# Retention, then a squared-ReLU layer: q of the first four pairs in 2 KB rows, clusters joined from the fifth group on, and the order planned anew

## The chip, the core and the metric

The kernel runs on one core of a Trainium2 chip. The metric is device time in microseconds of one execution, from the first instruction to the last. TensorE multiplies matrices, VectorE and ScalarE do elementwise work and read what TensorE leaves in PSUM, GpSimd does elementwise work in SBUF and issues some DMAs, and SyncE issues the other DMAs. Each engine takes its instructions in the order of the program and waits where an operand isn't there.

## The reference

```python
B, H, S, D = 8, 8, 576, 64
scores = (q @ k.transpose(0, 1, 3, 2)) / sqrt(D)
gamma = 1.0 - 2.0 ** (-5.0 - arange(H))
rel = pos[:, None] - pos[None, :]
Dmat = where(rel >= 0, gamma ** rel, 0.0)
x = (scores * Dmat) @ v                  # causal, with decay: retention
x = x.transpose(0, 2, 1, 3).reshape(B * S, H * D)      # 4608 x 512
out = (maximum(x @ w_in, 0.0) ** 2) @ w_out            # 512 -> 2048 -> 512
```

Inputs and output are float32. The kernel computes in float16 with float32 sums.

## The kernel before

**Units, groups, pairs.** The 4608 rows are cut into 36 units of 128 rows: 128 positions of one batch, or the last 64 positions of two batches (a tail). Two units make a group, so there are 18 groups. The first eight units, groups 0 to 3, are handled as four pairs: 256 neighbouring positions of one batch, named after their first unit (0, 2, 4, 6).

**Retention.** For each group: scores of k and q (`psc`), masked by VectorE into `rx` (pairs) or `rT` (later groups); sums of k times v (`psS`), from which VectorE makes the running states `stmp`, `R` and `Rm`; and outputs (`psO`) from the masked scores times v and q times the state. VectorE multiplies `psO` by the decay into `xT`, the input of the layer. These matmuls use quarter tiles of the array (64x64), so a cluster of them stands between full-tile matmuls, with a change before and after it.

**How k and q get transposed.** For pairs, k and q are loaded into `pair`, cast to float16 (`kx`, `qx`, two casts each), transposed by TensorE (`psT`) and copied to `kqT`. From unit 8 on, GpSimd casts them to `kq` and a DMA transposes `kq` into `kqT`. v is cast with a decay factor, to `vx` (pairs) or `v`.

**The layer.** `ph` is `xT` times w_in; ScalarE makes `rl` (ReLU) and mostly also the square `gT`; VectorE does a few squares. `po` is `gT` times w_out: plainly for group 0 (128x512 matmuls), and by a scheme of seven products instead of eight for the rest (128x256 matmuls, with `gS`, sums of `gT`, and `wT`, differences of w_out, made by VectorE).

**Loads.** All on the same DMA engines: k, q and v of pairs 0 and 2; then eight pieces of the weights, 512 KB each, issued by GpSimd (w0 to w3 of w_in, w4 to w7 of w_out); then pairs 4 and 6, k of pair 4 being held back by `behind` until w5 has landed; then units 8 and on. A pair's load is 512 KB. Before, partition p of all three held positions 2p and 2p+1 of each head, in runs of 512 bytes.

**What sets the order.** The program's order is not written by hand. A class `Schedule` plays the whole kernel through as a list of tasks, each with an engine, a key (smallest first among those ready), a duration, the resources that it takes, and its users; and emits the instructions of all engines in the order of that play. So a changed duration moves instructions on all engines. `LAG` adds to the landing times of some loads in that play, `WARM` is the number of matmuls on junk data that keep TensorE busy ahead of the real work, and `JOIN` says from which group on the output of one group and the scores of the next share a cluster:

```python
def joined(g):
    return JOIN <= g < last_g
...
f1: emit_out1(g); emit_scores(g + 1)     # q times the old state, and scores of the next group
f2: emit_sums(g + 1); emit_out2(g)       # sums of the next group, and the rest of the output
```

A group that is not joined runs scores and sums in one cluster and its output in another, with a drain between the output's halves. With JOIN at 5 the fifth group (number 4) is the last one of that kind, the final group aside.

Of the kernel before, what the change touches and what calls it, by code (L numbers as in the profile page):

```python
# [9 lines left out]
FP32 = mybir.dt.float32  # L10
# [5 lines left out]
class Schedule:  # L16
# [6 lines left out]

    def add(self, eng, key, dur, fn, deps=(), acq=(), after=None, lag=0.0):
        t = dict(eng=eng, key=key, dur=dur, fn=fn, acq=acq, n=len(self.tasks), users=[], free=[], lag=lag,
                 left=len(deps), ready=0.0, lat=self.LAT[eng] if after is None else after)
        for d in deps:
            d["users"].append(t)
        self.tasks.append(t)
        return t  # L30
# [11 lines left out]
    def emit(self):  # L42
        ready = {e: [] for e in self.LAT}
        busy = {e: False for e in self.LAT}
        events = []
        order = []
        seq = 0

        def push(at, what, t):
            nonlocal seq  # L50
            seq += 1
            heapq.heappush(events, (at, seq, what, t))
        for t in self.tasks:
            if t["left"] == 0:
                heapq.heappush(ready[t["eng"]], (t["key"], t["n"], t))
        now = 0.0
        while True:
            for e in ready:
                if busy[e]:
                    continue  # L60
                held = []
                while ready[e]:
                    item = heapq.heappop(ready[e])
                    t = item[2]
                    if all(self.count[r] >= t["acq"].count(r) for r in t["acq"]):
                        for r in t["acq"]:
                            self.count[r] -= 1
                        t["start"] = now
                        order.append(t)
                        busy[e] = True  # L70
                        push(now + t["dur"], "end", t)
                        break
                    held.append(item)
                for item in held:
                    heapq.heappush(ready[e], item)
            if not events:
                break
            now = events[0][0]
            while events and events[0][0] <= now + 1e-9:
                _, _, what, t = heapq.heappop(events)  # L80
                if what == "end":
                    busy[t["eng"]] = False
                    for w in t["users"]:
# [20 lines left out]
def kernel(  # L104
# [105 lines left out]

    mask2 = const.tile([P, 2, 2, 64], FP32, name="mask2")
    nc.gpsimd.memset(mask2, 1.0)
    for c in range(2):
        for e in range(2):
            m = mask2[c * 64:(c + 1) * 64, e]
            nc.gpsimd.affine_select(out=m, in_=m, compare_op=ALU.is_ge, fill=0.0, base=-e, pattern=[[1, 2], [2, 64]],  # L216
                                    channel_multiplier=-2)
# [6 lines left out]
    L = 2 * NF  # L224
    WARM = 34
    EARLY = 20
    SQ_ACT = (0, 1, 2, 3, 4, 5, 6)
    SPREAD = 0.1
    QL = 0.8
    BESIDE = 1.1  # L230
    PAUSE = 1.5
# [3 lines left out]
    SQ_LATE = (1, 4, 6)  # L235
    JOIN = 5
    LAG = {"k4": 0.7, "q4": 0.5}
    LAG_T, LAG_O = 1.5, 5.0
# [69 lines left out]
    def add_load_pair(name, u):  # L308
        n = "kqv".index(name)

        def fn():
# [3 lines left out]
            b, c = units[u][1:]  # L315
            t = nc.sync.dma_start(out=x, in_=(k, q, v)[n][b, :, c * P:(c + 2) * P, :].rearrange("h (p e) d -> p h (e d)", e=2))
            if (name, u) == ("k", 4):
                behind(t, tile_of["w", 5])
            tile_of["load", name, u] = t
        loaded[name, u] = loaded[name, u + 1] = dma_task(0, 1.81 if loaded else 2.9, fn, acq=("wst",) if name != "q" else (),  # L320
                                                         after=2.1 + LAG.get(name + str(u), 0.0))

    issues = []

    def add_weight(i):
# [9 lines left out]
        issues.append(issue)  # L335
        t = add("SP", 0, 2.75, lambda: None, deps=last_load + [issue], after=2.1 + LAG.get(f"w{i}", 0.0))
        last_load[:] = [t]
# [65 lines left out]
    def add_unit_pair(u, base):  # L403
# [4 lines left out]
        for i, name in enumerate("kqv"):  # L408
            xs[name] = []
            for e in range(2):  # L410
                eng = ("DVE" if (e if name == "v" else lead) else "ACT" if name == "k" and u >= 4 or u == 2 and e else
                       "DVE" if name == "q" and u == 2 else "POOL")

                def fc(name=name, e=e, eng=eng):
# [4 lines left out]
                    if name == "v":  # L419
                        (nc.vector if eng == "DVE" else nc.gpsimd).tensor_tensor(  # L420
                            out=t.rearrange("p (h d) -> p h d", d=D), in0=x,
                            in1=vdec[f"pair{e}"].rearrange("p (h o) -> p h o", o=1).to_broadcast([P, H, D]), op=ALU.mult)
                    else:
                        engines[eng](out=t.rearrange("p (n b a d) -> p n b a d", n=2, b=2, a=2),
# [9 lines left out]
        for i, name in enumerate("kq"):  # L434
# [9 lines left out]
            for s in range(2):  # L444
                on_act = i == 0 or s == 0 or u > 0

                def fe(i=i, s=s, on_act=on_act):
                    if i == 0:
                        tile_of["kqT", u + s] = work.tile([P, 2 * NP, P], FP16, name="kqT", tag="kqT", bufs=6)
                    (nc.scalar.copy if on_act else nc.vector.tensor_copy)(  # L450
                        out=tile_of["kqT", u + s][:, i * NP:(i + 1) * NP].rearrange("p x (e t) -> p e x t", e=2),
                        in_=tile_of["psT", u, i][:, :, :, half(s)])
                es.append(add("ACT" if on_act else "DVE", base + 3 + i + s / 2, 0.66, fe, deps=[t] + T["kqT", u + s],
# [14 lines left out]
    def add_ret_pair(g):  # L468
# [7 lines left out]
        for e in range(2):  # L476
# [11 lines left out]
            for a in range(2):  # L488
                def fm(e=e, a=a):
                    nc.vector.tensor_tensor(  # L490
                        out=rT[e][:, a], in0=rT["ps", e][a].rearrange("p (n i) -> p n i", i=P),
                        in1=mask2[:, e].rearrange("p (o e) i -> p o (e i)", o=1).to_broadcast([P, NP, P]), op=ALU.mult)
                ms.append(add("DVE", base + 5 + e, 0.66, fm, deps=[t] + ms))
# [79 lines left out]
        for s in range(2):  # L573
            def fx(s=s):
                if s == 0:
                    tile_of["x", g] = x_pool.tile([P, NP, 2 * P], FP16, name="xT", tag="xT")
                nc.vector.tensor_tensor(
                    out=tile_of["x", g][:, :, s * P:(s + 1) * P].rearrange("p n (i e) -> p n e i", e=2),
                    in0=tile_of["psO", g][s].rearrange("p (n e i) -> p n e i", n=NP, e=2),
                    in1=gam_f.rearrange("p n (i e) -> p n e i", e=2), op=ALU.mult)  # L580
            T["x", u + s] = add("DVE", base + 25 + s, 0.7, fx, deps=[t] + ([T["x", u]] if s else []), acq=() if s else ("x",))
# [119 lines left out]
    def after_sums(g, t, key, res):  # L701
# [23 lines left out]
        r1 = add("DVE", key + 0.2 - URGENT, 0.69, fr1, deps=[r0])  # L725
        r2 = add("DVE", key + 0.3, 0.65, fr2, deps=[r1], acq=("R",))
        T["Rm", g], T["R", g], T["Rread", g], T["Rmread", g] = r0, r2, [], r1
# [94 lines left out]
    def add_wT(i, in0, in1):  # L822
        ts = []
        for h in range(2):
            def f(h=h):
                sl = slice(h * HF // 2, (h + 1) * HF // 2)
                nc.vector.tensor_tensor(out=wT[i][:, sl], in0=in0[:, sl], in1=in1[:, sl], op=ALU.subtract)
            ts.append(add("DVE", WT_KEY + i, 0.7, f, deps=sum((wcast[j] for j in range(4, 8 if i else 6)), [])))
        return ts
# [5 lines left out]
    for x, y in ((t2, t1), (t4, t2)):  # L835
        for p in y:
            for w in x:
                sched.need(w, p)
    wT_done = {7: t3, 6: t2, 5: t1, 4: t4}
# [18 lines left out]
    def add_ff(g):  # L858
# [10 lines left out]
        for fb in range(NF // nf):  # L869
# [18 lines left out]
            def fg(fb=fb, on_act=on_act):  # L888
# [6 lines left out]
                else:  # L895
                    nc.vector.tensor_tensor(out=t, in0=rl, in1=rl, op=ALU.mult)  # L896
            r = add("ACT", place(4 * fb + 4), 0.6, fr, deps=[f1[-1]], acq=("rl",))
            sched.free("ff", [r])
            sq.append(add("ACT" if on_act else "DVE", place(4 * fb + 6), 0.63 if on_act else 0.55, fg, deps=[r] + sq[:1],
                          acq=() if fb else ("g",)))  # L900
            sched.free("rl", [sq[-1]])
# [30 lines left out]
    def add_strassen(g, us, base, sq):  # L932
# [7 lines left out]
        def add_sum(k, key, parts, in0, in1, op, deps, start=()):  # L940
            out_ = []
            for h in range(parts):
                def f(sl=cut(parts, h)):
                    if ("S", g) not in tile_of:
                        tile_of["S", g] = stage.tile([P, 4, HF, P], FP16, name="gS", tag="wst")
                    nc.vector.tensor_tensor(out=tile_of["S", g][:, k, sl], in0=in0(sl), in1=in1(sl), op=op)  # L946
                out_.append(add("DVE", key + h, (BESIDE if h else 0.5) if parts > 1 else 0.8, f, deps=deps(h, parts) + list(start)))
            sums[k] = out_
# [163 lines left out]
```

## Time and profile before

| | |
|---|---|
| time, median of 3 | 289.84 us (289.72 to 289.88) |
| span of the profiled execution | 288.5 us |
| TensorE busy | 280.7 us, 97% |
| ScalarE, VectorE, GpSimd busy | 187.5, 177.7, 87.1 us |
| DMA engines, share of the time by windows | 1.20 from 5 to 12 us, 0.97 from 100 to 200 us |
| matmuls of the layer, busy | ph 136.6 us; po in five groups, 135.8 us in sum |

Matmuls are pipelined: one of 128x256 is shown with 273 ns, but the next starts 109 ns after it. So the time of a stretch of matmuls is read from start to start, and a hole shows as a start that comes too late. The profile counts a stretch as idle from 150 ns on.

### The profile page before, as it was taken

The page shows a single profiled execution, that of the slowest core. Times are in us where ns is not written, and L with a number is a line of the kernel's source. Part 1 is how long each engine was busy: PE and PEld are TensorE (multiplying, and loading weights), DVE is VectorE, ACT ScalarE, POOL GpSimd, SP SyncE. Part 2 cuts the span into 40 slices and gives each one's busy share as a digit, 9 for nine tenths or more (in the row PEclk, how much of TensorE's full clock was granted, in tenths as well). Part 3 has the DMA queues.
Part 4 walks back from the last instruction along what each step waited for, and adds up shares of the span by engine and source line. Part 5 has one row for each costly group of instructions (what it writes and reads, how often), then busy time and mean ns, then how long its engine had stood idle before and what let it go on. Part 6 is the DMA issues. An engine that isn't in the chain of part 4 may idle for free.

```text
span 288.5 us, 10135 instructions
## 1 busy us (share of the span) xinstructions
PE 280.7 (97%) x4346; PEld 236.0 (82%) x4346; DVE 177.7 (62%) x341; ACT 187.5 (65%) x363; POOL 87.1 (30%) x124
## 2 busy tenths in 40 slices
PE   7999999999999999999999999999999999999994
PEld 2568767888888888888888888888888888888883
DVE  3772389868466756657666574767666566364632
ACT  5558975667584757667575748675848665847830
POOL 5660045433525243423325151534433100000000
PEclk9999999999999999999999999999999999999999
DMA  7999999999999898989898997989899420102004
GB/s 202 275 208 206 248 277 267 168 240 144 212 222 186 210 201 216 179 214 168 222 146 197 231 185 182 220 200 248 177 160 228 110 75 5 73 2 75 0 2 145
DMA packets 122156, 49.94 MB, mean 173 GB/s; under 512 B 94720, under 2 KB 117760, under 8 KB 122112
## 3 DMA queue, kind: packets, MB, share of 16 engines
q1 hardware_dynamic: 117568, 44.84, 71.0%
q0 software_dynamic: 4224, 4.19, 8.8%
q8 instruction: 34, 0.56, 0.8%
q10 hardware_dynamic: 320, 0.26, 0.4%
q14 instruction: 10, 0.08, 0.1%
HBM read 36.70 MB, written 9.44 MB: 160 GB/s over the span
## 4 chain that ended last, share of the span: by engine, by line
PE 88%; DMA 3%; DVE 3%; POOL 2%; issue 2%; DVEq 0%; POOLq 0%
PE ph L876 43%; PE po L973 36%; PE psO L357 4%; DMA w_in<-in_moe_w_in_dram 3%; PE po L916 2%; PE psS L357 2%; PE psc L357 2%; DVE rx L490 1%; DVE o L996 1%; DVE gS L946 1%; POOL mask L216 0%; DVE vx L420 0%; POOL vx L420 0%; POOL w_in L331 0%; PE psT L439 0%
## 5 line engine op out<-in xcount | busy, mean ns | idle before, releaser
L876 PE MATMUL ph<-xT,w_in 128*128 128x256 f16 x1152 | 136.6, 273 | 0.3 <-DMA w_in<-in_moe_w_in_dram 0.3
L876 PEld LDWEIGHTS <-w_in 128*128 128x128 f16 x1152 | 111.4, 98 | 14.7 <-DMA w_in<-in_moe_w_in_dram 0.6
L884 ACT ACTIVATE rl<-ph 128x512 f16<-128x512 f32 x144 | 84.3, 586 | 50.7 <-PE ph L876 48.1
L894 ACT ACTIVATE gT<-rl 128x512 f16<-128x512 f16 x118 | 74.4, 631 | 3.4
L973 PEld LDWEIGHTS <-gS 128*128 128x128 f16 x544 | 51.7, 98 | 6.5
L973 PE MATMUL po<-wT,gS 128*128 128x256 f16 x408 | 55.8, 273 | 0.0
L946 DVE TENSOR_TENSOR gS<-gT,gS 128x512 f16<-128x512 f16 (+1 forms) x51 | 31.3, 613 | 24.2 <-ACT gT L894 23.7
L973 PEld LDWEIGHTS <-gT 128*128 128x128 f16 x408 | 39.6, 98 | 4.8
L973 PE MATMUL po<-w_out,gT 128*128 128x256 f16 x272 | 36.8, 273 | 0.0
L387 POOL TENSOR_TENSOR v<-v,vdec_full 128x512 f16<-128x512 f32 x24 | 26.6, 1108 | 28.1 <-DMA v<-in_v_dram 24.4
L371 POOL CAST kq<-k 128x512 f16<-128x512 f32 x28 | 19.7, 702 | 36.9 <-DMA k<-in_k_dram 31.2
L946 DVE TENSOR_TENSOR gS<-gT 128x1024 f16<-128x1024 f16 x34 | 24.7, 726 | 6.4 <-ACT gT L894 6.3
L382 POOL CAST kq<-q 128x512 f16<-128x512 f32 x24 | 15.6, 649 | 32.0 <-DMA q<-in_q_dram 31.8
L896 DVE TENSOR_TENSOR gT<-rl 128x512 f16<-128x512 f16 x26 | 11.8, 455 | 20.1 <-ACT rl L884 20.1
L996 DVE TENSOR_TENSOR o<-po,u 128x256 f32<-128x256 f32 x33 | 13.9, 422 | 15.3 <-PE po L973 7.7
L986 ACT COPY u<-po 128x256 f32<-128x256 f32 x34 | 12.5, 368 | 15.7 <-PE po L973 15.5
L751 DVE TENSOR_TENSOR xT<-psO,gam_full 128x512 f16<-128x512 f32 x28 | 18.0, 685 | 3.8 <-PE psO L357 3.6
L996 DVE TENSOR_TENSOR o<-po,p 128x256 f32<-128x256 f32 x18 | 7.6, 424 | 20.6 <-ACT u L986 12.7
L973 PE MATMUL po<-w_out,gS 128*128 128x256 f16 x136 | 18.0, 273 | 0.0
L692 DVE TENSOR_TENSOR rT<-psc,mask_full 128x512 f16<-128x512 f32 x24 | 15.6, 685 | 3.7 <-PE psc L357 3.2
L973 PE MATMUL po<-wT,gT 128*128 128x256 f16 x136 | 17.6, 273 | 0.0
L1047 ACT COPY o<-po 128x256 f32<-128x256 f32 x16 | 5.9, 370 | 10.8 <-PE po L973 9.1
(82 smaller groups left out, 227.1 us busy)
## 6 DMA issues: line engine op xcount, KB each, us to landing
out_dram<-o SPq DMA_DIRECT2D x32, 256.0 KB, 3.0
k<-in_k_dram SPq DMA_DIRECT2D x24, 256.0 KB, 4.5
q<-in_q_dram SPq DMA_DIRECT2D x96, 64.0 KB, 3.2
v<-in_v_dram SPq DMA_DIRECT2D x24, 256.0 KB, 3.5
pair<-in_k_dram SPq DMA_DIRECT2D x4, 512.0 KB, 7.0
pair<-in_q_dram SPq DMA_DIRECT2D x4, 512.0 KB, 6.1
pair<-in_v_dram SPq DMA_DIRECT2D x4, 512.0 KB, 6.6
w_in<-in_moe_w_in_dram POOLq DMA_DIRECT2D x4, 512.0 KB, 9.2
```

Source lines behind the costliest of these rows:

```text
L357: t = nc.tensor.matmul(out_, lhsT=lhsT, rhs=rhs, start=start, stop=True, skip_group_check=True, tile_position=(64 * row, 64 * col))
L371: op(out=out_.rearrange("p (n b a d) -> p n b a d", n=2, b=2, a=2), in_=in_.rearrange("p (a n b) d -> p n b a d", n=2, a=2))
L382: nc.gpsimd.tensor_copy(out=tile_of["kq", u][:, 1].rearrange("p (t a d) -> p a t d", t=4, a=2), in_=tile_of["q32", u].rearrange("p (a t) d ...
L387: nc.gpsimd.tensor_tensor(out=t, in0=tile_of["v32", u], in1=vdec[kind].rearrange("p (h o) -> p h o", o=1).to_broadcast([P, H, D]), op=ALU. ...
L692: tile_of["masking", g] = nc.vector.tensor_tensor(out=tile_of["rT", g][:, :, a], in0=tile_of["psc", g][a].rearrange("p (s n i) -> p s n i" ...
L751: nc.vector.tensor_tensor(out=tile_of["x", g].rearrange("p n (s e i) -> p e (n s) i", s=n, e=2)[:, c], in0=y.rearrange("p (o t r) -> p o r ...
L876: nc.tensor.matmul(tile_of["ph", g, fb][:, j, :], lhsT=w_in16[:, m, fi * P:(fi + 1) * P], rhs=tile_of["x", g][:, m, :], start=(m == 0), st ...
L884: nc.scalar.activation(out=t, in_=tile_of["ph", g, fb], func=ACTF.Relu)
L894: nc.scalar.activation(out=t, in_=rl, func=ACTF.Square)
L946: nc.vector.tensor_tensor(out=tile_of["S", g][:, k, sl], in0=in0(sl), in1=in1(sl), op=op)
L973: nc.tensor.matmul(tile_of["pb", g, bank], lhsT=left(i), rhs=right[:, i, :], start=(start and i == 0), stop=(i == HF - 1), skip_group_chec ...
L996: nc.vector.tensor_tensor(out=o_tile(u)[:, half * HM:(half + 1) * HM], in0=bank(x), in1=tile_of[name, g], op=ALU.add)
```

## The change

**q of the pairs.** The eight heads are split in two halves of four, and each half is one DMA: partition p holds 8 neighbouring positions of one head, p = 4 * (block of 8 positions) + head within the half. Each row is 2 KB in one run. The positions of q are thereby in another order, so the cast to `qx`, the copy of q to `kqT`, the mask `mask2` and the write of `xT` take other strides. k and v are loaded as before.

**Join.** JOIN goes from 5 to 4, so group 4 shares clusters with group 5.

**Order.** The planner gets other figures: VectorE's operations with two SBUF operands (`soft`) run at a `SHARED` rate of 0.22 beside a long GpSimd task, and faster otherwise; loads of q, weights and some landings have other durations; the differences `wT` are released half by half; `HURRY` puts a few tasks of group 1 first; and there are 26 warm-up matmuls instead of 34. For pair 2, ScalarE now does all casts of k and q, where GpSimd, VectorE and ScalarE shared them.

```diff
-    def add(self, eng, key, dur, fn, deps=(), acq=(), after=None, lag=0.0):
+    SHARED = 0.22
+    def add(self, eng, key, dur, fn, deps=(), acq=(), after=None, lag=0.0, soft=False):
...
+        def shared(beside):
+            t = port["task"]
+            if t is not None:
+                port["left"] -= (now - port["at"]) * (self.SHARED if port["beside"] else 1.0)
+                port["at"] = now
+                t["end"] = now + max(port["left"], 0.0) / (self.SHARED if beside else 1.0)
+                push(t["end"], "end", t)
+            port["beside"] = beside
...
-    WARM = 34
+    WARM = 26
-    BESIDE = 1.1
+    HURRY = 60
-    JOIN = 5
-    LAG = {"k4": 0.7, "q4": 0.5}
+    JOIN = 4
+    LAG = {"k0": 0.3, "w7": 1.4, "v6": 1.2}
...
-            t = nc.sync.dma_start(out=x, in_=(k, q, v)[n][b, :, c * P:(c + 2) * P, :].rearrange("h (p e) d -> p h (e d)", e=2))
+            src = (k, q, v)[n][b, :, c * P:(c + 2) * P, :]
+            if name == "q":
+                for a in range(2):
+                    t = nc.sync.dma_start(out=x[:, NP * a:NP * a + NP].rearrange("p t d -> p (t d)"),
+                                          in_=src.rearrange("(a x) (r t) d -> a r x (t d)", a=2, t=8)[a])
+            else:
+                t = nc.sync.dma_start(out=x, in_=src.rearrange("h (p e) d -> p h (e d)", e=2))
...
-        loaded[name, u] = loaded[name, u + 1] = dma_task(0, 1.81 if loaded else 2.9, fn, ...
+        loaded[name, u] = loaded[name, u + 1] = dma_task(0, 2.9 if not loaded else 1.41 if name == "q" else 1.81, fn, ...
...
-        t = add("SP", 0, 2.75, lambda: None, deps=last_load + [issue], after=2.1 + LAG.get(f"w{i}", 0.0))
+        t = add("SP", 0, 2.58, lambda: None, deps=last_load + [issue], after=3.0 + LAG.get(f"w{i}", 0.0))
...
-                eng = ("DVE" if (e if name == "v" else lead) else "ACT" if name == "k" and u >= 4 or u == 2 and e else
-                       "DVE" if name == "q" and u == 2 else "POOL")
+                eng = ("DVE" if (e if name == "v" else lead) else "ACT" if name == "k" and u >= 4 or u == 2 and name != "v" else "POOL")
...
+                    elif name == "q":
+                        x = tile_of["q32", u].rearrange("p (a t) (s d) -> p a (t s) d", a=2, s=2)[:, :, NP * e:NP * e + NP]
+                        engines[eng](out=t.rearrange("p (t a d) -> p a t d", t=NP, a=2), in_=x)
...
+                    out_, in_ = tile_of["kqT", u + s][:, i * NP:(i + 1) * NP], tile_of["psT", u, i]
+                    if i == 0:
+                        out_, in_ = out_.rearrange("p x (e t) -> p e x t", e=2), in_[:, :, :, half(s)]
+                    else:
+                        out_ = out_.rearrange("p x (t r) -> p t x r", r=16)
+                        in_ = in_.rearrange("p e y (r x) -> p (e y) x r", x=NP)[:, :, :, 16 * s:16 * s + 16]
...
-                    out=tile_of["x", g][:, :, s * P:(s + 1) * P].rearrange("p n (i e) -> p n e i", e=2),
-                    in0=tile_of["psO", g][s].rearrange("p (n e i) -> p n e i", n=NP, e=2),
+                    out=tile_of["x", g][:, :, s * P:(s + 1) * P].rearrange("p n (r t) -> p n r t", t=8),
+                    in0=tile_of["psO", g][s].rearrange("p (n t r) -> p n r t", n=NP, t=8),
...
-            ts.append(add("DVE", WT_KEY + i, 0.7, f, deps=sum((wcast[j] for j in range(4, 8 if i else 6)), [])))
+            ts.append(add("DVE", WT_KEY + i, 0.68, f, deps=wcast[4 + h] + (wcast[6 + h] if i else []), soft=True))
```

More of the change, by code (lines that the diff above doesn't have):

```diff
@@ L22, in __init__ @@
         self.tasks = []
-    def add(self, eng, key, dur, fn, deps=(), acq=(), after=None, lag=0.0):
-        t = dict(eng=eng, key=key, dur=dur, fn=fn, acq=acq, n=len(self.tasks), users=[], free=[], lag=lag,
+    SHARED = 0.22
+    def add(self, eng, key, dur, fn, deps=(), acq=(), after=None, lag=0.0, soft=False):
+        t = dict(soft=soft, eng=eng, key=key, dur=dur, fn=fn, acq=acq, n=len(self.tasks), users=[], free=[], lag=lag,
                  left=len(deps), ready=0.0, lat=self.LAT[eng] if after is None else after)
@@ L56, in emit @@
         now = 0.0
+        port = dict(task=None, left=0.0, at=0.0, beside=False)
+        def shared(beside):
[6 more added lines that the diff above has]
+            port["beside"] = beside
         while True:
@@ L70, in emit @@
                         busy[e] = True
-                        push(now + t["dur"], "end", t)
+                        t["end"] = now + t["dur"]
+                        if t["soft"]:
+                            port.update(task=t, left=t["dur"], at=now)
+                            shared(port["beside"])
+                        else:
+                            push(t["end"], "end", t)
+                        if e == "POOL" and t["dur"] > 0.5:
+                            shared(True)
                         break
@@ L81, in emit @@
                 if what == "end":
+                    if abs(t["end"] - now) > 1e-6:
+                        continue
+                    t["end"] = -1.0
                     busy[t["eng"]] = False
+                    if t["soft"]:
+                        port["task"] = None
+                    elif t["eng"] == "POOL" and t["dur"] > 0.5:
+                        shared(False)
                     for w in t["users"]:
@@ L209 @@
                                     compare_op=ALU.is_ge, fill=0.0, base=0, pattern=pattern, channel_multiplier=-1)
-    mask2 = const.tile([P, 2, 2, 64], FP32, name="mask2")
+    mask2 = const.tile([P, 2, 8, 16], FP32, name="mask2")
     nc.gpsimd.memset(mask2, 1.0)
@@ L215 @@
             m = mask2[c * 64:(c + 1) * 64, e]
-            nc.gpsimd.affine_select(out=m, in_=m, compare_op=ALU.is_ge, fill=0.0, base=-e, pattern=[[1, 2], [2, 64]],
+            nc.gpsimd.affine_select(out=m, in_=m, compare_op=ALU.is_ge, fill=0.0, base=-e, pattern=[[1, 8], [8, 16]],
                                     channel_multiplier=-2)
@@ L319, in fn @@
             tile_of["load", name, u] = t
-        loaded[name, u] = loaded[name, u + 1] = dma_task(0, 1.81 if loaded else 2.9, fn, acq=("wst",) if name != "q" else (),
+        loaded[name, u] = loaded[name, u + 1] = dma_task(0, 2.9 if not loaded else 1.41 if name == "q" else 1.81, fn, acq=("wst",) if name != "q" else (),
                                                          after=2.1 + LAG.get(name + str(u), 0.0))
@@ L449, in fe @@
                         tile_of["kqT", u + s] = work.tile([P, 2 * NP, P], FP16, name="kqT", tag="kqT", bufs=6)
-                    (nc.scalar.copy if on_act else nc.vector.tensor_copy)(
-                        out=tile_of["kqT", u + s][:, i * NP:(i + 1) * NP].rearrange("p x (e t) -> p e x t", e=2),
-                        in_=tile_of["psT", u, i][:, :, :, half(s)])
+                    out_, in_ = tile_of["kqT", u + s][:, i * NP:(i + 1) * NP], tile_of["psT", u, i]
+                    if i == 0:
+                        out_, in_ = out_.rearrange("p x (e t) -> p e x t", e=2), in_[:, :, :, half(s)]
+                    else:
+                        out_ = out_.rearrange("p x (t r) -> p t x r", r=16)
+                        in_ = in_.rearrange("p e y (r x) -> p (e y) x r", x=NP)[:, :, :, 16 * s:16 * s + 16]
+                    (nc.scalar.copy if on_act else nc.vector.tensor_copy)(out=out_, in_=in_)
                 es.append(add("ACT" if on_act else "DVE", base + 3 + i + s / 2, 0.66, fe, deps=[t] + T["kqT", u + s],
@@ L491, in fm @@
                         out=rT[e][:, a], in0=rT["ps", e][a].rearrange("p (n i) -> p n i", i=P),
-                        in1=mask2[:, e].rearrange("p (o e) i -> p o (e i)", o=1).to_broadcast([P, NP, P]), op=ALU.mult)
+                        in1=mask2[:, e].rearrange("p (o t) r -> p o (t r)", o=1).to_broadcast([P, NP, P]), op=ALU.mult)
                 ms.append(add("DVE", base + 5 + e, 0.66, fm, deps=[t] + ms))
@@ L577, in fx @@
                 nc.vector.tensor_tensor(
-                    out=tile_of["x", g][:, :, s * P:(s + 1) * P].rearrange("p n (i e) -> p n e i", e=2),
-                    in0=tile_of["psO", g][s].rearrange("p (n e i) -> p n e i", n=NP, e=2),
-                    in1=gam_f.rearrange("p n (i e) -> p n e i", e=2), op=ALU.mult)
+                    out=tile_of["x", g][:, :, s * P:(s + 1) * P].rearrange("p n (r t) -> p n r t", t=8),
+                    in0=tile_of["psO", g][s].rearrange("p (n t r) -> p n r t", n=NP, t=8),
+                    in1=gam_f.rearrange("p n (r t) -> p n r t", t=8), op=ALU.mult)
             T["x", u + s] = add("DVE", base + 25 + s, 0.7, fx, deps=[t] + ([T["x", u]] if s else []), acq=() if s else ("x",))
@@ L725, in after_sums @@
         r1 = add("DVE", key + 0.2 - URGENT, 0.69, fr1, deps=[r0])
-        r2 = add("DVE", key + 0.3, 0.65, fr2, deps=[r1], acq=("R",))
+        r2 = add("DVE", key + 0.3, 0.62, fr2, deps=[r1], acq=("R",), soft=True)
         T["Rm", g], T["R", g], T["Rread", g], T["Rmread", g] = r0, r2, [], r1
@@ L835 @@
     for x, y in ((t2, t1), (t4, t2)):
-        for p in y:
-            for w in x:
-                sched.need(w, p)
+        for w, p in zip(x, y):
+            sched.need(w, p)
     wT_done = {7: t3, 6: t2, 5: t1, 4: t4}
@@ L896, in fg @@
                     nc.vector.tensor_tensor(out=t, in0=rl, in1=rl, op=ALU.mult)
-            r = add("ACT", place(4 * fb + 4), 0.6, fr, deps=[f1[-1]], acq=("rl",))
+            r = add("ACT", place(4 * fb + 4) - HURRY * (g == 1 and fb == 7), 0.6, fr, deps=[f1[-1]], acq=("rl",))
             sched.free("ff", [r])
-            sq.append(add("ACT" if on_act else "DVE", place(4 * fb + 6), 0.63 if on_act else 0.55, fg, deps=[r] + sq[:1],
-                          acq=() if fb else ("g",)))
+            sq.append(add("ACT" if on_act else "DVE", place(4 * fb + 6) - HURRY * (g == 1 and not on_act), 0.63 if on_act else 0.43, fg, deps=[r] + sq[:1],
+                          acq=() if fb else ("g",), soft=not on_act))
             sched.free("rl", [sq[-1]])
@@ L946, in f @@
                     nc.vector.tensor_tensor(out=tile_of["S", g][:, k, sl], in0=in0(sl), in1=in1(sl), op=op)
-                out_.append(add("DVE", key + h, (BESIDE if h else 0.5) if parts > 1 else 0.8, f, deps=deps(h, parts) + list(start)))
+                out_.append(add("DVE", key + h - HURRY * (g == 1), 0.43 if parts > 1 else 0.72, f, deps=deps(h, parts) + list(start), soft=True))
             sums[k] = out_
```

## The prediction

> **What bounds the kernel now.** I read the page first, for shares; then the list of who waited for whom on the matmul engine; then the chain of waits in the one stretch that is not solid; then the timelines of the engines that feed it.
>
> ```profile
> PE 280.7 (97%) x4346; PEld 236.0 (82%) x4346; DVE 177.7 (62%) x341; ACT 187.5 (65%) x363; POOL 87.1 (30%) x124
> PE   7999999999999999999999999999999999999994
> PEclk9999999999999999999999999999999999999999
> ```
>
> TensorE is the bound, at full clock, and no other engine comes near. So an edit is worth only what it takes from the matmul stream or from the holes in it. All of TensorE's holes are early:
>
> ```profile
> PE psT L439 <- DVE kx L424: 0.8, 1, 0.8
> PE psS L357 <- POOL vx L420: 0.3, 1, 0.3
> PE ph L876 <- DMA w_in<-in_moe_w_in_dram: 0.3, 1, 0.3
> PE psS L357 <- DVE vx L420: 0.3, 1, 0.3
> ```
>
> The first two lie before 12 us, where warm-up matmuls are run anyway. The third is where real work begins. The timeline of TensorE there, and of GpSimd, which issues the weight DMAs:
>
> ```profile
> 17.73 1.92 PE L876 MATMUL ph<-xT,w_in 128*128 128x256 f16 x16
> 19.97 1.48 PE L876 MATMUL ph<-xT,w_in 128*128 128x256 f16 x12 [0.33 <-DMA w_in<-in_moe_w_in_dram]
> ```
> ```profile
> 10.94 0.81 POOL L331 DMA_DIRECT2D w_in<-in_moe_w_in_dram  x1
> ```
> ```profile
> DMA to landing us min/median/max: 9.0/9.0/9.0
> ```
>
> The second piece of w_in is issued at 10.94 and lands 9.0 us later, at 19.94; TensorE restarts at 19.97. From there to 49.3 it never stops, so the date of that landing sets all that follows. The wait has nothing to do with the issue: six loads are ahead of the weights, and the windows view has the DMA engines full (share 1.20 and 290 GB/s from 5 to 12 us, 207 GB/s of weights from 14 to 32 us).
>
> The fourth hole is in the chain of waits:
>
> ```profile
> 43.33 0.44 PE psS L357 x32
> ...
> 47.18 0.68 DVE rx L490
> 47.86 0.33 DVE o L996
> 48.19 0.60 DVE gS L946
> 48.79 1.03 DVE vx L420
> 49.81 0.04 issue
> 49.86 0.41 PE psS L357 x28
> ```
>
> Here the chain leaves TensorE for 6 us of VectorE work: R, stmp, four rx masks, and only then vx of pair 6, for which psS of group 3 waits. Start to start, the fourth psS matmul costs 0.52 us more than its neighbours, and one psc after it (50.96) 0.16 more. After 51 us every start-to-start step is either a plain matmul (109 ns for 128x256) or the change between full and quarter tiles.
>
> **What the Trainium skill says.** "DMA: Bandwidth & Descriptors", section "Why small descriptors are slow (HBM only)", names a fixed cost per packet and per descriptor, so longer runs move faster. The trace agrees: 512-byte loads move at 299 GB/s (3 to 12 us), while the two stretches filled by 2 KB stores show 380 and 366 GB/s. "GPSIMD Engine Reference", the table that lists SBUF interfaces, has GpSimd and VectorE share theirs when VectorE has two SBUF inputs. The trace agrees: the gS subtraction of 1024 takes 0.68 us alone and 1.53 beside a GpSimd multiply at 68.27; the first qx cast at 39.05 took 0.86 instead of 0.61 beside gS. "TensorE: Matmul & The Clock Gate", section "What's actually happening", has the array fall to half clock after an idle window of about 3.4 us; here only the start shows it (11 warm-ups in 4.32 us, 0.39 each, against 0.22 later). "VectorE: DVE Perf Modes", section "Mode 2×_1P", wants step 1 for packed 16-bit reads, which bears on one small copy below.
>
> **The change part by part.** Total matmul work is the same; only eight warm-ups go. I compared the order of instructions of both kernels engine by engine.
>
> *q0 and q2 in 2 KB rows.* Each 512 KB load of 512-byte rows takes 1.8 us (landings at 4.99, 6.78, 8.59, 10.39). In 2 KB rows it is 256 packets; the stores' packets took 87 to 90 ns each, so 256 x 88 / 16 = 1.4 us; by rate, 0.524 MB at 366 GB/s is 1.43. The two q loads ahead of the weights save 2 x 0.4 = 0.8 us (0.4 to 0.9). Every weight piece queues behind them and lands earlier by that: the restart moves from 19.97 to 19.2. For this, the matmuls before must be ready: xT of group 0 ended at 15.95 against a first ph at 17.73, and the masks of group 1 at 19.94 against psO at 21.39. Both have more than 0.8 us in hand, and q's casts of pair 2 moved to ScalarE have it idle there. One kqT copy on VectorE now reads with step 4; it may go from 0.42 to the 0.68 of an unpacked read. That 0.26 lies in the same slack. **-0.8.**
>
> *The order between 22 and 42 us.* In the new order psT of k4 and q4 is moved ahead of eight of the po matmuls of 512 (8 x 0.216 = 1.73), and psT of q4 also ahead of ten po of 256 (10 x 0.109 = 1.09). So TensorE asks for qx of pair 4 2.82 us earlier, relative to the restart. Before, the two GpSimd casts ended at 40.52 (39.05 plus 1.47) and psT began at 41.85: slack 1.33. The shortfall is 2.82 - 1.33 = 1.49, about 1.52 with a release of 0.03. What comes back: q4 itself is 0.4 shorter, and the casts may need 2 x 0.61 = 1.22 instead of 1.47. The restart's 0.8 cancels, since k4 is queued behind w5 and moves with it. This leaves 1.52 - 0.4 - 0.25 = 0.87 us in which TensorE stands, with po, psS and all later work behind it in its queue (bounds: 0, if pair 4 gets more of the DMA engines beside the last weights; 1.1, if q4 gains only 0.3 and the casts stay slow). k's casts on ScalarE ended at 39.11 against psT at 40.31; 1.73 earlier they are short by 0.5, but they waited for ScalarE until 37.97 with k4 landed at 37.08, and the new order puts them right behind the last rl. I count them at nothing. **+0.87.**
>
> *psS of group 3.* Between psS of group 2 and of group 3 stand now 46 po of 256 and two of 512, where there were 24 of 256; and VectorE does the masks straight after stmp, then xT, o and vx. From psS of group 2: 1.1 us of R and stmp, masks to about 4.2, R and wT to 5.3, xT after psO to 7.0, o and vx to about 8.3; TensorE needs about 9.3. The hole of 0.52 and the 0.16 go. **-0.68.**
>
> *More cuts.* psc now stands alone where it followed psO, so there is one more change to quarter tiles and back: 0.09 + 0.14. **+0.24.** Joining from group 4 merges its clusters with those of group 5, but the number of clusters from group 4 on stays 28; what goes is the drain between its halves (0.27 at 68.07). **-0.27.**
>
> *The rest.* Masks, xT and casts with other strides keep their counts of elements and their f32 PSUM reads (0.68 each); xT and rx are off the path by the paragraphs above. The planner's new figures for shared SBUF access change no instruction. The last 220 matmuls stand in the old order. Cost nothing.
>
> Sum: -0.8 + 0.87 - 0.68 + 0.24 - 0.27 = -0.64, so 289.84 - 0.64 = **289.2 us**.
>
> **The rivals.** (a) *q4 is in time.* The 0.87 falls away: 288.3. For it: the last weights and pair 4 share the engines, and whichever gets more decides; q4 needs only 0.9. Against: bytes queued before the end of q4 are fixed. (b) *The load gain is small and the stall full.* q saves 0.2 each: -0.4 + 1.1 - 0.4 + 0.24 - 0.27 = +0.3 at the worst, 289.6 to 290.1: no difference. For it: stores are not loads. (c) *A new wait, slower.* Joining group 4 asks for psc of group 5 at about 71 us instead of 77.3, and its DMA transpose (issued 67.83, others land 4 to 5.5 us after issue) was done at about 72. It moves with the loads, by some 1.6 us, to about 70.5. If it moves by 0.4 only, TensorE stands about 1.1 us more, and groups 6, 7 and 9 have similar dates (transposes landed 2 to 3 us ahead of psc before): 290.5 to 291. Or the eight missing warm-ups let the clock fall: half speed for some 3.4 us costs 1.7, to 290.9; against it, the idle time I find before the first ph is 1 to 2 us. (d) *Better than (a)*, below 288.2: the loads save 0.46 each and nothing stalls.
>
> **How the numbers follow.** The forecast, 288.9 to 289.6: 0.42. (a): 0.32. (b): 0.14. (c): 0.08. (d): 0.04. The bound of 0.2% is 0.58 us, so 289.26: a little over half of the forecast, all of (a) and (d) are faster, 0.58; the rest of the forecast and (b), same, 0.34; (c), slower, 0.08. The range leaves out (d), the better edge of (a), (c) and the worse edge of (b): 288.2 to 289.9.
>
> **What would show it.** Right: q's pair loads land about 1.4 us after k's; the ph behind the wait for w_in starts near 19.2; psT of q4 shows idle time of about 0.9 us put down to GpSimd's qx; no idle time before psS of group 3; nothing on TensorE after 55 us. Wrong: a restart still near 20; no idle time before psT; a wait at psc for a transpose in groups 5 to 9; matmuls of 128x256 slower than 109 ns after 17 us.

## The result, and the profile after

The changed kernel takes **291.87 us** (median of 4, 291.70 to 292.75) against 289.86 for the kernel before beside it: ratio 1.0074, 95% interval 1.0053 to 1.0096. It is slower by 2.0 us, where 289.2 was forecast, and outside the range. A second set of 22 executions, below, gave 1.0065 (1.0043 to 1.0087). The ratios are taken over undisturbed executions and are not simply the quotient of the two medians.

The page of the changed kernel, TensorE's line and its two rows of slices, answers to the first lines shown of before:

```profile
PE 280.1 (97%) x4338; PEld 236.0 (81%) x4338; DVE 177.9 (61%) x340; ACT 188.8 (65%) x365; POOL 86.8 (30%) x123
PE   6989999999999899999999999999999999999994
PEclk9979999999999999999999999999999999999999
```

TensorE is still the bound with the same work. Two things matter: a 7 in the third slice of the clock (with an 8 for TensorE there), and an 8 in the fourteenth slice of TensorE, 94 to 101 us, far behind 55 us, where I had expected nothing. Four lines of who waited for whom on TensorE (us in total, times, longest):

```profile
PE psc L390 <- DMA kqT<-kq: 0.7, 1, 0.7
PE psc L390 <- issue: 0.7, 1, 0.7
PE psS L390 <- DVE vx L452: 0.6, 1, 0.6
PE psS L390 <- POOL vx L452: 0.4, 1, 0.4
```

The wait of `ph` for `w_in` is gone in this execution (it is back in the second profile below), and a wait of `psc` for a DMA transpose has come. The restart, in TensorE's timeline, and GpSimd's issue of the second and third piece of w_in:

```profile
17.15 0.25 PE L390 MATMUL psc<-kqT 64*64 64x128 f16 x3 [0.72 <-issue]
17.33 4.90 PE L914 MATMUL ph<-xT,w_in 128*128 128x256 f16 x28
22.16 0.35 PE L390 MATMUL psO<-rx,vx 64*64 64x128 f16 x10
```
```profile
11.04 1.55 POOL L364 DMA_DIRECT2D w_in<-in_moe_w_in_dram  x2
```

The second piece is issued at 11.04 and lands at 19.22 (before: 19.94), so the loads did gain 0.7 us. But 28 `ph`, which need 28 x 0.109 = 3.05 us at full clock, take 4.90. The windows view says why (columns: TensorE, weight loads, VectorE, ScalarE, GpSimd busy, then the granted clock, DMA share, GB/s). Two lines of before, then those of the changed kernel:

```profile
15.00:16.00 1.00, 0.96 (x37) 0.54 (x34) 0.95 (x2) 0.80 (x2) 1.00 (x2) 1.00 1.24 211
16.00:17.00 1.00, 1.00 (x19) 0.33 (x8) 0.83 (x2) 0.28 (x1) 1.00 (x2) 1.00 1.24 203
```
```profile
15.00:16.00 1.00, 0.40 (x41) 0.40 (x44) 1.00 (x2) 0.05 (x1) 1.00 (x2) 1.00 1.19 198
16.00:17.00 1.00, 0.43 (x32) 0.27 (x20) 1.00 (x3) 0.00 (x0) 1.00 (x3) 1.00 1.25 205
17.00:18.00 1.00, 0.85 (x8) 0.67 (x9) 1.00 (x3) 0.00 (x0) 1.00 (x2) 0.86 1.24 204
18.00:19.00 1.00, 1.00 (x7) 0.71 (x5) 0.97 (x3) 0.08 (x1) 0.38 (x1) 0.50 1.25 209
...
20.00:21.00 1.00, 1.00 (x6) 0.72 (x5) 0.68 (x2) 0.55 (x2) 0.00 (x0) 0.50 1.30 222
```

TensorE was busy 0.4 us in each of two microseconds, and then ran at half clock until just after 21 us: a cold stretch, as I call it below. It costs about 1.7 us. The other place is the chain of waits from 80 to 98 us, which ends in the wait for `kqT`:

```profile
84.01 0.38 ACT u L1024
...
84.41 0.43 DVE o L1034
84.85 0.18 SPq L883
...
86.29 1.44 SPq L325
...
90.13 3.14 DMA v<-in_v_dram
...
93.43 0.22 POOL v L420
93.65 4.03 DMA kqT<-kq
97.68 0.04 issue
97.72 0.28 PE psc L390 x9
```

Read it backwards: scores of group 7 wait for a transpose that took 4.03 us, which was issued once GpSimd had cast a v that landed at 93.27; that load stood in SyncE's queue behind other loads and an output store (L883), which had waited for its tile. `psc` stands 0.92 us longer than its neighbours at 96.80, and 0.24 at 84.15 (group 6). Before, the scores of group 7 ran without a stop:

```profile
98.94 0.43 PE L357 MATMUL psc<-kqT 64*64 64x64 f16 x32
```

The hole before `psS` of group 3 is gone, as forecast; a small one, 0.18 us, stands nearby, behind ScalarE's `u` at 50.22. Pair 4 shows no stall in this execution: TensorE was already late by the cold stretch.

### The profile page after: what moved, and what is told of

Same layout as the page of the kernel before. It is cut to its first block, busy times and chain, and to the rows that moved or that the text cites. A ratio compares the mean times of both kernels' runs of the same rounds, so it can differ in the third digit from the quotient of the medians.

```text
span 290.0 us, 10127 instructions
## 1 busy us (share of the span) xinstructions
PE 280.1 (97%) x4338; PEld 236.0 (81%) x4338; DVE 177.9 (61%) x340; ACT 188.8 (65%) x365; POOL 86.8 (30%) x123
## 4 chain that ended last, share of the span: by engine, by line
PE 88%; DMA 5%; DVE 3%; SPq 2%; issue 1%; ACT 0%; POOL 0%; DVEq 0%; POOLq 0%
PE ph L914 43%; PE po L1011 34%; PE psO L390 4%; PE po L954 2%; DMA pair<-in_v_dram 2%; PE psc L390 2%; PE psS L390 2%; DMA kqT<-kq 1%; SPq L325 1%; DMA v<-in_v_dram 1%; DVE rx L529 1%; PE psT L474 1%; DVE R L500 1%; DVE vx L452 0%; DVE o L1034 0%
## 5 line engine op out<-in xcount | busy, mean ns | idle before, releaser
L914 PE MATMUL ph<-xT,w_in 128*128 128x256 f16 x1152 | 138.6, 275 | 0.0
L1011 PE MATMUL po<-wT,gS 128*128 128x256 f16 x408 | 54.6, 273 | 0.0
L984 DVE TENSOR_TENSOR gS<-gT,gS 128x512 f16<-128x512 f16 (+1 forms) x51 | 30.1, 591 | 18.9 <-ACT gT L932 18.2
L420 POOL TENSOR_TENSOR v<-v,vdec_full 128x512 f16<-128x512 f32 x24 | 27.4, 1143 | 26.1 <-DMA v<-in_v_dram 24.0
L984 DVE TENSOR_TENSOR gS<-gT 128x1024 f16<-128x1024 f16 x34 | 27.2, 800 | 6.8 <-ACT gT L932 5.6
L404 POOL CAST kq<-k 128x512 f16<-128x512 f32 x28 | 18.3, 655 | 35.4 <-DMA k<-in_k_dram 31.7
L415 POOL CAST kq<-q 128x512 f16<-128x512 f32 x24 | 16.2, 676 | 37.1 <-DMA q<-in_q_dram 36.8
L500 DVE TENSOR_TENSOR R<-stmp,dec 128x512 f16<-128x512 f32 (+1 forms) x18 | 12.0, 665 | 0.5
```

The source lines that it names most:

```text
L404: op(out=out_.rearrange("p (n b a d) -> p n b a d", n=2, b=2, a=2), in_=in_.rearrange("p (a n b) d -> p n b a d", n=2, a=2))
L415: nc.gpsimd.tensor_copy(out=tile_of["kq", u][:, 1].rearrange("p (t a d) -> p a t d", t=4, a=2), in_=tile_of["q32", u].rearrange("p (a t) d ...
L420: nc.gpsimd.tensor_tensor(out=t, in0=tile_of["v32", u], in1=vdec[kind].rearrange("p (h o) -> p h o", o=1).to_broadcast([P, H, D]), op=ALU. ...
L914: nc.tensor.matmul(tile_of["ph", g, fb][:, j, :], lhsT=w_in16[:, m, fi * P:(fi + 1) * P], rhs=tile_of["x", g][:, m, :], start=(m == 0), st ...
L1011: nc.tensor.matmul(tile_of["pb", g, bank], lhsT=left(i), rhs=right[:, i, :], start=(start and i == 0), stop=(i == HF - 1), skip_group_chec ...
```

## The experiments

Four theories. **1:** the clock, through the missing warm-ups. **2:** joining group 4 asks for scores before their transposes have landed. **3:** pair 4's casts are late for `psT` and `psS`. **4**, formed after eight runs: the new load figures in the plan are behind both 2 and 3. Each kernel is compared with the kernel before, run beside it; its own median there moved between 289.81 and 290.49 us, so the ratios count.

**Warm-ups back**, in the changed kernel:

```diff
-    WARM = 26
+    WARM = 34
```


> The changed kernel with 34 warm-up matmuls instead of 26, nothing else. Theory 1 (the missing warm-ups let TensorE's clock fall to half at 18 us, which costs 1.7 us): the clock stays full from 17 to 22 us, the first 28 ph take about 3.1 us instead of 4.9, and the time is 290.2 us or so, 1.7 below the changed kernel. Theory 2 (scores of groups 5 to 9 are asked for before their DMA transposes have landed): the clock is full, but TensorE comes to those scores 1.7 us earlier and waits that much longer, so psc of groups 6 and 7 wait 2 to 3 us in sum, where they waited 1.16, and the time stays at 291.5 to 292. A stall of psT of pair 4 of about 0.9 us, hidden by the cold stretch, would show between 37 and 41 us.

291.20 us, ratio 1.0039 (1.0025 to 1.0052). The clock stays full in all seven executions, and `psO` of group 1 starts at 20.94 instead of 22.16. But the gain is 0.3% or so, 0.7 to 1.0 us, and not 1.7, and the kernel is still slower than before. In its profile `psT` of q4 stands 0.33 us and between k4 and q4 0.20 more, `psS` of group 2 0.42 for GpSimd's `vx` (beyond the 0.31 that this change to quarter tiles took without a wait in the first profile, at 41.33), and `psc` of group 9 0.48 for its transpose. Neither theory is enough alone.

**JOIN 5**, in the changed kernel:

```diff
-    JOIN = 4
+    JOIN = 5
```


> The changed kernel with clusters joined from group 5 on (JOIN 5, as in the kernel before), all else as changed, order planned anew. Theory 2 (joining group 4 asks for the scores of groups 5 to 9 about 2 to 4 us of TensorE's work earlier than before): the waits of psc of groups 6 and 7 for the transpose go, and the time falls by 1 to 1.5 us, to 290.4 to 290.9. Theory 1 (clock): nothing changes in the first 20 us, so the time stays at 291.5 to 292.

290.82 us, 1.0044 (1.0024 to 1.0064): the interval overlaps that of the changed kernel, so a gain by JOIN 5 isn't shown. In its profile the wait at groups 6 and 7 goes; pair 4 waits 0.33 (`psT`) and 0.48 (`psS`). This profile shows something else as well, in its windows view:

```profile
15.00:16.00 1.00, 0.44 (x44) 0.44 (x47) 1.00 (x2) 0.00 (x0) 1.00 (x2) 1.00 1.19 197
16.00:17.00 1.00, 0.39 (x29) 0.23 (x17) 1.00 (x3) 0.00 (x0) 1.00 (x3) 1.00 1.26 206
17.00:18.00 1.00, 0.82 (x9) 0.70 (x10) 1.00 (x3) 0.00 (x0) 1.00 (x2) 1.00 1.23 203
```

Nearly the same idle time as in the changed kernel, and the clock stays full: these shares alone don't decide whether it falls. What does is open. Here 6 of 14 executions show a mean clock of 0.994 or less.

**q in 2 KB rows alone**, in the kernel before: the load, the cast to `qx`, the copy to `kqT`, the mask and `xT` as in the change, and nothing else.

> The kernel before with q of the pairs in 2 KB rows (its casts, copy, mask and xT with their strides), and nothing else of the change: the planner's figures, JOIN and the warm-ups are as before. If the gain of the loads is real and passed on: w1 lands 0.7 us earlier, TensorE restarts at 19.3, and the time is 289.1 us (0.7 below before), where the casts of pair 4 keep up. If the restart moves but the gain is lost at a later wait for data (k4 and q4, or the masks before psS of group 3): 289.6 to 289.9. If the new strides cost something on the path: above 290.

290.01 us, 1.0010 (0.9994 to 1.0026): no difference. TensorE's timeline at the restart:

```profile
16.84 0.59 PE L256 MATMUL warm<-wT 128*128 128x512 f16 x2
17.37 0.64 PE L363 MATMUL psc<-kqT 64*64 64x128 f16 x32
17.94 3.23 PE L889 MATMUL ph<-xT,w_in 128*128 128x256 f16 x28
21.10 0.64 PE L363 MATMUL psO<-rx,vx 64*64 64x128 f16 x32
```

In this execution the second piece of w_in lands at 18.80, 1.1 us earlier than before, and the 28 `ph` run without a hole; yet `psO` starts at 21.10 against 21.39. The first `ph` is no earlier than before (17.94 against 17.73): it stands behind warm-ups and scores in TensorE's own queue. So with this order only the hole of before was to be had there, 0.33 us by the profile, 0.49 from start to start.

**26 warm-ups**, in the kernel before:

```diff
-    WARM = 34
+    WARM = 26
```


> The kernel before with 26 warm-up matmuls instead of 34, nothing else. Theory 1: with eight warm-ups less the clock falls near 18 us in some or all executions, the first 28 ph take up to 1.7 us longer, and the time is up to 291.5. Theory 2: the warm-ups matter nothing, since the kernel before is busy enough from 12 to 17 us; the time stays at 289.8.

290.17 us, 1.0018 (1.0002 to 1.0033). Of 22 executions, 7 show a clock of 0.994 or less; their median is 291.61, that of the other 15 is 289.96. So executions with a low clock take 1.65 us longer here, which fits the cold stretch, and they are about a third.

**The changed kernel again**, for more executions.

> The changed kernel, unchanged, for more executions of it. Theory 1 (by chance of its phase, the clock drops near 17 us in some executions): a good third of the executions show a mean clock of 0.994 or less, as 7 of 22 did with 26 warm-ups in the kernel before. Theory 2 (the other waits take the place of the cold stretch when it stays away): the executions at full clock are no faster than the others, 291.5 to 292.5; if the clock alone made the loss, they are at 290.2.

292.40 us (290.57 to 295.85, 22 executions). Nine are at a clock of 0.994 or less, median 293.44; the thirteen at full clock have 292.22, far above before's 290.49. The clock is not the main loss. The profile is of an execution at full clock; it shows a wait for the third piece of w_in, the waits of pair 4, and that of group 9:

```profile
PE ph L914 <- DMA w_in<-in_moe_w_in_dram: 0.9, 1, 0.9
```
```profile
39.51 0.40 PE L474 MATMUL psT<-ident,qx 128*128 128x128 f16 x4 [0.17 <-POOL qx L457]
39.74 1.46 PE L954 MATMUL po<-w_out,gT 128*128 128x512 f16 x6
41.52 0.45 PE L390 MATMUL psS<-vx,kx 64*64 64x64 f16 x32 [0.32 <-POOL vx L452]
```
```profile
121.91 0.30 PE L390 MATMUL psc<-kqT 64*64 64x64 f16 x16
123.46 0.32 PE L390 MATMUL psc<-kqT 64*64 64x64 f16 x16 [1.25 <-DMA kqT<-kq]
```

Start to start the waits are 1.03 (at 22.78), 0.33, 0.39 and 1.44 us. The third piece landed at 22.73, against 22.43 before and 21.76 in the first profile: the gain of the loads isn't there in every execution. And group 9, which waits here, did not wait in the first profile, where group 7 did: the place of the wait differs between two executions of one kernel.

**JOIN 4 alone**, in the kernel before:

```diff
-    JOIN = 5
+    JOIN = 4
```


> The kernel before with JOIN 4, nothing else; its plan asks for scores of group 5 1.7 us of TensorE's work earlier than before, group 6 0.9 earlier, group 9 1.7 earlier. Theory 2 (joining group 4 asks for scores ahead of their DMA transposes): psc of groups 6 to 9 wait for kqT from DMA, 0.5 to 1 us in sum, and the time is 290.4 or more. If joining is harmless by itself and only the order that the other figures make does the harm: no such wait, 289.6 to 289.9.

290.10 beside 290.49 us, 0.9998 (0.9971 to 1.0024), and no wait for `kqT` from DMA in the profile. Joining costs nothing that shows with the old figures, and theory 2, as I had put it, falls.

**34 warm-ups and JOIN 5** in the changed kernel:

> The changed kernel with 34 warm-ups and JOIN 5 both. If the clock and the early scores are all of the loss, the two gains (0.67 by warm-ups alone, 1.05 by JOIN alone) add up, and the time is 290.1 or below, with no wait for kqT from DMA and no cold stretch. Theory 3 (what is left is pair 4: psT of q4 and psS of group 2 moved ahead of po matmuls, so that they wait for GpSimd's casts): 0.5 to 1.1 us of waits for qx and vx remain between 37 and 42 us, and the time stays at 290.2 to 290.6.

291.42 beside 290.49 us, 1.0016 (0.9996 to 1.0037). Waits remain: 0.08 and 0.33 at `psT` of q4, 0.42 at `psS` of group 2, and, against both expectations, 1.13 at `psc` of group 9 for its transpose, with JOIN 5.

**And pair 4 later in the plan:**

```diff
-    LAG = {"k0": 0.3, "w7": 1.4, "v6": 1.2}
+    LAG = {"k0": 0.3, "w7": 1.4, "v6": 1.2, "k4": 1.7, "q4": 1.7, "v4": 1.0}
```


> As the run before (34 warm-ups, JOIN 5), and the landings of pair 4 put later in the plan (LAG of k4 and q4 1.7, of v4 1.0), so that psT of q4 stands 1.7 us and psS of group 2 2.2 us of TensorE's work later than in the changed kernel. Theory 3: the waits for qx and vx at 37 to 42 us go, and the time is 0.5 to 1 lower than without, 289.4 to 289.8. If pair 4's waits are not what is left: no gain over the run before.

290.83 beside 290.49 us, 1.0003 (0.9979 to 1.0027). The waits of pair 4 are gone; 0.51 at `psS` and 0.53 at `psc` of group 3 have come, group 7 waits 0.29 for its transpose, and group 9 still 1.05. The medians moved by about the forecast half microsecond, but the intervals overlap: theory 3 has the waits right and leaves group 9 unexplained.

What the changed kernel and all these forms of it share, and the kernel before has not, is where the plan puts the scores: between the first `ph` and the scores of group 9 stand 744 matmuls of 128x256, before 776. These 32 are 3.5 us of TensorE's work at 0.109 each. In the source, three lines could do that to loads and all that follows them. So theory 4.

**The load figures alone**, in the kernel with q in 2 KB rows:

```diff
-    LAG = {"k4": 0.7, "q4": 0.5}
+    LAG = {"k0": 0.3, "w7": 1.4, "v6": 1.2}
...
-        ... dma_task(0, 1.81 if loaded else 2.9, fn, ...
+        ... dma_task(0, 2.9 if not loaded else 1.41 if name == "q" else 1.81, fn, ...
...
-        t = add("SP", 0, 2.75, ..., after=2.1 + ...)
+        t = add("SP", 0, 2.58, ..., after=3.0 + ...)
```


> The kernel before with q in 2 KB rows and the changed planner's figures for loads (q 1.41, weights 2.58 and 3.0, the new LAG); warm-ups 34, JOIN 5 and all other figures as before. Its order has psT of q4 3.0, psS of group 2 2.6, psc of groups 6, 7 and 9 3.1, 3.1 and 3.5 us of TensorE's work earlier than with q in 2 KB rows alone. Theory 4 (the new load figures make the plan think that pairs and transposes land 2 to 3 us sooner, and TensorE is sent to them too early): waits for qx and vx of pair 4 and for kqT from DMA at groups 6 to 9, and 290.5 to 291.3, 0.7 to 1.5 above q in 2 KB rows alone. If the loss needs JOIN 4 or the shared-port figures: 289.7 to 290.

291.47 us, 1.0049 (1.0029 to 1.0069), against 1.0010 without them. JOIN 5, 34 warm-ups and the old VectorE figures don't protect it. The timeline of one of its longer executions (292.83) has the same two waits among smaller ones, 0.32 us start to start at pair 4 and 0.99 at group 8:

```profile
40.25 0.40 PE L448 MATMUL psT<-ident,qx 128*128 128x128 f16 x4
40.81 0.40 PE L448 MATMUL psT<-ident,qx 128*128 128x128 f16 x4 [0.16 <-POOL qx L431]
...
110.75 0.30 PE L363 MATMUL psc<-kqT 64*64 64x64 f16 x16
111.85 0.32 PE L363 MATMUL psc<-kqT 64*64 64x64 f16 x16 [0.80 <-DMA kqT<-kq]
```

**The changed kernel with the old load figures** (the same three lines, back), all else as changed:

> The changed kernel with the planner's figures for loads as they were (q 1.81, weights 2.75 and 2.1, LAG of k4 and q4), all else as changed: JOIN 4, 26 warm-ups, shared-port figures, HURRY, q in 2 KB rows. Its order has psT of q4, psS of group 2 and the scores of groups 5 to 9 nearly where the kernel before had them. Theory 4: no wait for qx, vx or kqT from 37 us on, and executions at full clock take 289.6 to 290.1; the cold stretch near 17 us can still come in a third of them and add 1.7. If the load figures aren't the cause: as the changed kernel, 291.5 to 292.4.

**289.31 us, 0.9972 (0.9955 to 0.9988)**: faster than both kernels. Three lines that carry no instruction are worth 1.0065 - 0.9972 = 0.93% here, about 2.7 us. Hardly any of it is the clock: at full clock the changed kernel had 292.22 beside 290.49, and these nineteen executions have 289.15 beside 289.89. (Three are at 0.993 or less, 290.66 to 293.56.) But theory 4 had said that no wait for `kqT` would be left. The profile, of the slowest execution, 293.56, with a cold stretch from 18.2 to 21.6 us, has one:

```profile
PE psc L390 <- DMA kqT<-kq: 1.3, 1, 1.3
```

It stands at group 10: asked at 137.77, landed at 139.23, 1.50 us from start to start. So the old figures make such waits rarer or shorter; they don't exclude them.

**And with 34 warm-ups and JOIN 5:**

> As the run before, and with 34 warm-ups and JOIN 5: what remains of the change is q in 2 KB rows, the shared-port figures, HURRY, the halves of wT and the casts of pair 2. Theory 4: no cold stretch, no wait from 37 us on, slack of 1 to 2 us and more between the landing of the transposes and their scores: 289.4 to 289.8, the same as the kernel before or a little below. If the shared-port figures cost something of their own, above 290.

289.71 us, 0.9992 (0.9975 to 1.0009); no wait for `kqT` anywhere, and all executions at full clock. It equals the kernel before, and the 289.4 to 289.8 expected. So the figures for the shared port, HURRY, the halves of `wT` and the casts of pair 2 cost nothing that shows. The load figures are worth less in this company: 1.0016 with the new ones (34 warm-ups, JOIN 5), 0.9992 with the old, and the intervals overlap.

**And with 34 warm-ups, JOIN 4:**

> The changed kernel with the old load figures in the plan and 34 warm-ups; JOIN 4 and all else as changed; its order from the first ph on is that of the kernel with the old load figures and 26 warm-ups. Theory 1 (the missing warm-ups let the clock fall in some executions): none at 0.994 or below, where that kernel had 3 in 22 (290.7 to 293.6), and the median is 289.1 us, that of its executions at full clock. If the eight warm-ups only shift work to the stretch ahead of ph: 289.3 or more.

289.65 beside 290.46 us, 0.9982 (0.9967 to 0.9998). No execution is cold; but the median is not below that with 26 warm-ups, and the intervals overlap. Eight warm-ups seem to guard against the fall of the clock (0 of 22 against 3 of 22); a gain in time by them isn't shown with this plan. Beside the changed kernel with 34 warm-ups and the new load figures (1.0039) the old ones are worth 0.57%, and here the intervals are apart. What TensorE waits for in this kernel, from the first `psT` on:

```profile
PE psT L474 <- DVE kx L459: 0.4, 1, 0.4
PE psc L390 <- DVE kqT L491: 0.4, 1, 0.4
PE psS L390 <- POOL vx L452: 0.2, 1, 0.2
PE psS L390 <- DVE vx L452: 0.2, 1, 0.2
```

No `kqT` from DMA and no `qx` is left in that list; start to start, 0.14 us shows at group 7, whose transpose landed at 96.59, 0.20 us after it was asked for.

## Why the prediction was wrong, point by point

The time by which TensorE asks for the scores of group 9, and the landing of the last transpose that they need, in us from the start of each profiled execution:

| kernel | load figures | asked | landed | wait |
|---|---|---|---|---|
| before | old | 125.25 | 122.58 | 0 |
| q in 2 KB rows | old | 124.46 | 119.72 | 0 |
| JOIN 4 alone | old | 123.30 | 121.87 | 0 |
| changed, old figures, 34, JOIN 5 | old | 123.01 | 120.70 | 0 |
| changed, old figures (cold) | old | 126.57 | 124.49 | 0 |
| changed, JOIN 5 | new | 121.91 | 122.03 | 0.06 |
| changed, 34 | new | 121.91 | (goes on at 122.51) | 0.48 |
| changed, 34, JOIN 5 | new | 121.74 | 122.94 | 1.13 |
| changed, 34, JOIN 5, pair 4 later | new | 121.66 | 122.78 | 1.05 |
| changed, second profile | new | 121.91 | (goes on at 123.46) | 1.44 |

For group 9, TensorE asks 1.4 us or more after the landings under the old figures, and ahead of them under the new ones. (Without a wait there: the first profile of the changed kernel, 1.7 us late by the cold stretch, and the load figures in the kernel with q in 2 KB rows, late by earlier waits; their waits are at groups 7 and 8.) The landings scatter by some three microseconds among the old ones alone, cold execution aside; those under the new figures are no earlier, but at the late end. The plan's new figures take 4 x 0.40 + 8 x 0.17 = 2.96 us off the stream of loads. In the profile the last pair load lands 2.1 us earlier (44.26 against 46.38), and the transposes not at all: the second one of groups 5 to 9 is issued at 68.1, 79.1, 93.7, 106.5 and 118.9, before at 67.8, 79.6, 92.5, 105.5 and 118.5. So the plan sends TensorE to scores up to 3.5 us of work earlier for data that comes when it came before. The new figures are not even wrong for the weights: their eight pieces land 2.57 us apart after and 2.60 before, nearer to 2.58 than to 2.75. As I read it, the old figures' error was the reserve.

- **The step that failed: the later groups, put at nothing.** "*Joining from group 4 merges its clusters [...] but the number of clusters from group 4 on stays 28*", and then "nothing on TensorE after 55 us". I costed the later groups by cuts and drains alone, and took the transposes to move "with the loads, by some 1.6 us". They moved by nothing, and TensorE came to them early: `psc` waits 0.24 and 0.92 us at groups 6 and 7 in the first profile, 1.44 at group 9 in the second. These are the waits of my rival (c), which had a chance of 0.08; but its 290.5 to 291 was too little even without the clock, since executions at full clock have 292.22 beside 290.49. And its cause, joining, costs nothing that shows alone. The cause is three figures in the plan that I had looked at only for their effect from 22 to 42 us; they are worth 0.93% in the changed kernel, less in other company.
- **q in 2 KB rows, -0.8.** Right in kind for the loads: w1 lands 0.7 and 1.4 us earlier in the two profiles of the changed kernel, 1.1 with q in 2 KB rows alone. Mis-sized for TensorE: with q in 2 KB rows alone about 0.3 at `psO` of group 1, and no difference in time. "Both have more than 0.8 us in hand" was true of `xT` and the masks; TensorE's queue ahead of the first `ph` had nothing in hand.
- **Order from 22 to 42 us, +0.87.** Right in kind and near in size: 0.33 and 0.39 us in the second profile of the changed kernel, though the larger part is `psS` waiting for `vx`, which I hadn't named, and not `psT` waiting for `qx`. In a cold execution it is hidden.
- **`psS` of group 3, -0.68.** Right: no wait there after.
- **More cuts +0.24, drain -0.27.** Too small to be tested apart; JOIN 4 alone is at 0.9998. (0.09 + 0.14 is 0.23.)
- **The clock.** I gave the idle time before the first `ph` as 1 to 2 us against a fall that wants some 3.4, and took that as safe: the second term put at nothing. The Trainium skill ("TensorE: Matmul & The Clock Gate", section "What's actually happening") speaks of an idle window of about 3.4 us; the trace differs: two microseconds in which TensorE was still busy 0.40 and 0.43 were enough in the first profile. Nine of 22 executions of the changed kernel have a low clock.
- **The copy of q to `kqT`**, 0.42 to 0.68: measured 0.68. `psc` of group 0 waits 0.28 us for it at 10.12, among the warm-ups.

Open: why landings scatter by so much, and whether stores that wait in SyncE's queue ahead of loads (the chain at 84.85) add to it; that was not tried. Nor was each of the three load figures tried alone on the chip, or the shared-port figures. And the rows of the table are one execution each: how the loss comes about is read from them, while its size rests on the ratios.

## What to carry to other kernels

When an order is planned from durations, a change of a duration is a change of every later date: compare, for each wait that crosses from a DMA to the bounding engine, the date of the ask with the date of the landing, all through the kernel, and not only where code changed. A plan with exact mean durations can leave the bounding engine no reserve against landings that scatter; here going back to the longer figures was worth 2.7 us in the changed kernel, and 0.7 to 1.7 us (0.24 to 0.57%) in the three other forms tried. And a change that makes loads faster gains only what TensorE stood still for them, which is read from start to start, not what the load gains.

## What the hardware showed that I had not expected

- TensorE's granted clock fell to 0.50 for about 3.4 us after two microseconds in which it was busy 0.40 and 0.43, and stayed at 1.00 in an execution with 0.44 and 0.39 (JOIN 5). Executions with a low clock took 1.65 us longer in the kernel before with 26 warm-ups (median of 7 against 15), 1.2 in the changed kernel and 0.6 with JOIN 5.
- The last DMA transpose of group 9 landed between 119.7 and 122.9 us (cold execution aside) in kernels whose loads up to there are the same bytes. Part of that is the issue: it was issued at 115.8 for the first of these and at 119.5 for the last, so it took 3.9 and 3.5 us.
